# Attention and mixture of depths in one kernel: ranks by one compare, first keys in parts, picks, sums and stores in another order

## The chip, the cores and the metric

The kernel runs on one core of a Trainium2 chip. The metric is the device time of one launch in microseconds (us). Before the change six runs lie between 436.78 and 439.22, median 437.97. The engines of the core work side by side and wait for each other through semaphores: TensorE (PE; its weight loads are shown apart as PEld), VectorE (DVE), ScalarE (ACT), GpSimd (POOL) and SyncE (SP). SP, ACT and POOL also issue DMA transfers, which 16 DMA engines carry out.

## The reference, cut to what matters

All data are float32. With B=8, H=12, S=448, Dh=64, D=768, F=1024, capacity 128:

```python
scores = scale * q @ k.T - log(S)            # for each of 96 heads
attn_out = sigmoid(scores) @ v
x = attn_out as (B, S, H*Dh)
scores = einsum('bsd,d->bs', x, w_gate)      # one gate score per token
out = x.copy()
for b in range(B):
    top_idx = the 128 tokens of 448 with the largest scores[b]
    xe = x[b, top_idx]
    ye = relu(xe @ w1) @ w2
    out[b, top_idx] = xe + sigmoid(scores[b, top_idx])[:, None] * ye
```

## The kernel before, in words

**Attention.** Four heads make a quad; a batch is three quads, so there are 24 quads, handled in pairs: 12 steps s, two quads (x = 0, 1) each. A step has seven slots n = 0..6. In a slot, `score` puts the products of 64 keys and all queries of each head into PSUM with 32x64 tiles of PE, `squash` turns them into sigmoids on ACT (two ACTIVATEs of about 1.0 us), and `value` multiplies earlier sigmoids by v. Scores of one slot and values of earlier slots alternate on PE. In step 0 there are no older values, and the first four slots (0 to 3) hold scores alone: slots 0 and 1 use quad 0, slots 2 and 3 quad 1. In step 0 keys are paired by `chunks` and `column`: pair c < 5 is blocks c and c+5 (a block is 32 tokens), the last four blocks make two pairs of their own.

**Layout.** `load` brings q and k of a quad with a token's row index t and r apart (token = 14 t + r); `turn` transposes 32x32 blocks on DVE, so that the head dimension lies on partitions. `load_v` brings v of both quads of a step: from step 6 on by ACT's queue, issued in slot 3 when the values of the step before are done, because one buffer serves them all; its first use is in slot 4.

**End of a step.** In slot 3 the values of step s-1 are complete. From step 4 on `after(s, 3)` then calls `block(s)`: `takes` (four DVE transposes that free PSUM), the work of the token network listed in `BLOCKS[s]`, which PE does in one go, and then the transposes of the next q and k. In a block, `("t", b)` is `turn_rows`: PE transposes the 128 picked rows of batch b; `(1, p, key)` and `(2, p, key)` are products of the two layers for a pair p of batches. The seven keys are the seven products of a Strassen scheme, which needs sums of weight quarters: `make_sum` builds one on DVE (`MADE` says after which slot), `keep_sum` stores it to DRAM through SP's queue (`KEPT`), `lend` reloads it to a place that is free then (`LENT`).

**Picking rows.** When a batch's output is complete, `gate_part` multiplies a quad's rows by the gate weights and reduces; `gate` adds up, transposes and writes 448 scores to DRAM, `gate_own` keeps each partition's own scores in `who`; `spread` reads the scores back to all partitions (`rep`); `ranking` counts for every token how many scores are above its own: per group of tokens c (`rank`, four groups) one compare with `is_gt` into `above`, and one `is_equal` times the mask `earlier` into `level`. `place` adds both, transposes, writes the ranks to DRAM with four DMAs and reads them back to all partitions (tile `hot`). `fetch` compares the ranks with the partition number, which gives token index and score of each pick, and `gather` fetches the rows of `out` by an indirect DMA. All these DMAs are POOL's; for the last batch SP issues those of `gate`, `spread` and `place`. `RANKED` and `FETCHED` say after which slot; `(5, 3): 1` and others at slot 3 run inside `block`, right after `takes`. `ranking` of odd batches runs in `after(s, 3)` of the step behind.

**Order.** The whole program is emitted by hand (`manual_schedule`): each engine and each queue works off its instructions in the order of the calls. A DMA issue also waits until an earlier DMA of the hardware queues gave back its semaphore.

**The end.** `rest` runs the last products. For batches 6 and 7 (p = 3), `fetch(7)` gathers the last rows, `("t", 7)` turns them, and after the second layer's sums (`second_sums`) `scatter` writes 128 rows back by an indirect DMA.

Of the kernel before, what the change touches and what calls it, by code (L numbers as in the profile page):

```python
# [17 lines left out]
def kernel(  # L18
# [20 lines left out]
    NF = 3  # L39
# [13 lines left out]
    QK_SCALE = 1.0 / math.sqrt(Dh)  # L53
    NEG_LOG_S = -math.log(S)
# [35 lines left out]
    def load(which, *quads):  # L90

        for i in quads:
            if i >= NQ:
                return
            if which == "q":
                t = heads["q", i] = head.tile([P, TB * Dh], F32, name="qT")
            elif i in (1, 2):
                if i == 1:
                    both = heads["both"] = moe.tile([P, 6 * KH * P], F32, name="rows_t")
                t = heads["both"][:, (i - 1) * TB * Dh:i * TB * Dh]  # L100
            else:
                t = head.tile([P, TB * Dh], F32, name="raw_k", bufs=1)
# [4 lines left out]
            heads[which, i] = t  # L107

# [22 lines left out]
    NA = NU - 2  # L131

# [8 lines left out]
    def load_v(s):  # L141
# [4 lines left out]
        if s in (1, 3):  # L146
# [5 lines left out]
        raw_v[s] = t = t.rearrange("p (h c) -> p h c", h=4)  # L152
# [6 lines left out]
        for m in range(4):  # L159
            y, odd = divmod(m, 2)  # L160
            rows = slice(m * TT, (m + 1) * TT)
            if s:
                (nc.scalar if s > 5 else nc.sync).dma_start(
                    out=t[rows], in_=block(y, odd * NU, NU))
            else:
                nc.sync.dma_start(out=t[rows, :, :NA * Dh], in_=block(y, odd * NA, NA))
                nc.sync.dma_start(out=t[rows, :, NA * Dh:],
                                  in_=block(1 - y, 2 * NA + 2 * odd, 2))
# [53 lines left out]
    def keep_sum(m, key):  # L222
# [5 lines left out]
    MADE = {(5, 4): (1, 5), (5, 5): (1, 7), (5, 6): (1, 6), (6, 4): (1, 3),  # L228
            (6, 6): (2, 5), (7, 0): (2, 6), (7, 4): (2, 7), (7, 5): (2, 4)}
    KEPT = {(6, 0): [(1, 5), (1, 7)], (6, 1): [(1, 6)], (6, 5): [(1, 3)],  # L230
            (7, 0): [(2, 5)], (7, 1): [(2, 6)], (7, 5): [(2, 7)], (7, 6): [(2, 4)]}
# [39 lines left out]
    earlier = const.tile([P, NC, S], mybir.dt.uint8, name="earlier")  # L271
# [4 lines left out]
    above = const.tile([P, NC], F32, name="above")  # L276
    level = const.tile([P, NC], F32, name="level")
# [3 lines left out]
    def constants():  # L281
# [10 lines left out]
        nc.gpsimd.memset(above, float(S))  # L292
        nc.gpsimd.memset(level, 0.0)
        for t in (gate_s, place_s, *who):
            nc.gpsimd.memset(t, 0.0)
        mine = moe.tile([P, NC], F32, name="place")
        for a in range(4):
            nc.gpsimd.iota(mine[a * TT:(a + 1) * TT], pattern=[[1, NC]], base=a * NC,
                           channel_multiplier=TB, allow_small_or_imprecise_dtypes=True)
        nc.gpsimd.iota(tokens, pattern=[[1, TB], [TB, TT]], base=0, channel_multiplier=0,  # L300
                       allow_small_or_imprecise_dtypes=True)
        for c in range(NC):
            nc.gpsimd.tensor_scalar(
                out=earlier[:, c, :], in0=tokens.rearrange("p r t -> p (r t)"),
# [740 lines left out]
```

## Time and profile before

| what | us |
|---|---|
| median of six runs | 437.97 |
| the profiled execution, device time | 439.67 |
| its span on the core, first to last instruction | 437.9 |
| PE busy | 423.1 |
| DVE busy | 298.8 |
| ACT busy | 190.7 |
| POOL busy | 52.6 |
| DVE on the two compares of `rank` (L466 and L469; 28 of 32 of each, the last batch is listed apart) | 18.9 and 19.1 |

The profile lists instructions by line of the kernel. A busy PE is not a PE at its full pace: its matmuls overlap, so a matmul that waits for its operands can still lie under the tail of the one before it. Its idle time is therefore a lower bound on what it lost. "Landing" of a DMA is the moment at which its semaphore is complete.

### The profile page before, as it was taken

The page shows a single profiled execution, that of the slowest core. Times are in us where ns is not written, and L with a number is a line of the kernel's source. Part 1 is how long each engine was busy: PE and PEld are TensorE (multiplying, and loading weights), DVE is VectorE, ACT ScalarE, POOL GpSimd, SP SyncE. Part 2 cuts the span into 40 slices and gives each one's busy share as a digit, 9 for nine tenths or more (in the row PEclk, how much of TensorE's full clock was granted, in tenths as well). Part 3 has the DMA queues.
Part 4 walks back from the last instruction along what each step waited for, and adds up shares of the span by engine and source line. Part 5 has one row for each costly group of instructions (what it writes and reads, how often), then busy time and mean ns, then how long its engine had stood idle before and what let it go on. Part 6 is the DMA issues. An engine that isn't in the chain of part 4 may idle for free.

```text
span 437.9 us, 14311 instructions
## 1 busy us (share of the span) xinstructions
PE 423.1 (97%) x6326; PEld 248.9 (57%) x6326; DVE 298.8 (68%) x640; ACT 190.7 (44%) x249; POOL 52.6 (12%) x87
## 2 busy tenths in 40 slices
PE   7999999999998999989999999999999899999995
PEld 3555453535673477455447438646545649768952
DVE  4318467865959975984998566765786768994472
ACT  3766666666653633640660562463263330102000
POOL 6000000210111020020021110010011110101001
PEclk9999999999999999999999999999999999999998
DMA  8786738889944997699649798299875960722001
GB/s 242 223 276 182 234 88 186 183 173 241 278 142 110 231 298 184 167 229 300 185 125 278 238 208 171 88 250 246 211 261 123 193 229 25 148 58 72 37 0 72
DMA packets 114361, 78.64 MB, mean 180 GB/s; under 512 B 91356, under 2 KB 100316, under 8 KB 114300
## 3 DMA queue, kind: packets, MB, share of 16 engines
q1 hardware_dynamic: 107548, 62.70, 54.6%
q0 software_dynamic: 3296, 9.54, 8.0%
q10 hardware_dynamic: 3456, 5.51, 5.0%
q8 instruction: 49, 0.80, 0.7%
q14 instruction: 12, 0.10, 0.1%
HBM read 57.25 MB, written 20.48 MB: 178 GB/s over the span
## 4 chain that ended last, share of the span: by engine, by line
PE 72%; DVE 11%; DMA 10%; issue 3%; ACT 3%; ACTq 1%; POOLq 0%; POOL 0%; SPq 0%; DVEq 0%
PE o L377 26%; PE a L348 26%; PE o L561 7%; PE o L625 5%; PE a L625 4%; DMA raw_v<-in_v_dram 3%; PE a L561 2%; DMA xe<-out_dram,idx 2%; DMA hot<-ranks 2%; ACT attn L362 1%; DVE scr L469 1%; DVE scr L466 1%; DVE scr L493 1%; DVE hidden L574 1%; DVE gate_p L412 1%
## 5 line engine op out<-in xcount | busy, mean ns | idle before, releaser
L348 PE MATMUL a<-qT,kT 32*64 32x448 f32 x2624 | 242.1, 537 | 0.1
L362 ACT ACTIVATE attn<-a,bias_s 128x896 f32<-128x896 f32 x162 | 161.5, 1007 | 84.0 <-PE a L348 81.2
L377 PE MATMUL o<-attn,raw_v 32*64 32x448 f32 x1952 | 175.2, 536 | 0.8 <-DMA raw_v<-in_v_dram 0.6
L348 PEld LDWEIGHTS a<-qT,kT 32*64 32x64 f32 x2624 | 93.9, 131 | 88.4 <-ACT attn L362 52.5
L377 PEld LDWEIGHTS o<-attn,raw_v 32*64 32x64 f32 x1952 | 67.2, 131 | 33.4 <-issue 26.6
L401 DVE STREAM_TRANSPOSE x_b<-o 128x448 f32<-128x448 f32 x48 | 28.1, 626 | 42.3 <-PE o L377 26.1
L377 PE MATMUL o<-attn,rows_t 32*64 32x448 f32 x448 | 42.1, 538 | 0.6 <-issue 0.6
L577 ACT ACTIVATE hidden<-hidden 128x512 f32<-128x512 f32 x12 | 7.5, 630 | 69.2 <-DVE hidden L574 69.2
L412 DVE TENSOR_REDUCE gate_p<-scr 128x14 f32<-128x448 f32 x48 | 29.8, 622 | 1.7
L574 DVE TENSOR_TENSOR hidden<-o,hidden 128x512 f32<-128x512 f32 x23 | 15.2, 687 | 22.4 <-PE o L561 22.2
L409 DVE TENSOR_TENSOR scr<-x_b,wg_b 128x448 f32<-128x448 f32 x48 | 29.4, 612 | 1.0
L329 DVE STREAM_TRANSPOSE kT<-raw_k 128x448 f32<-128x448 f32 x42 | 24.1, 611 | 8.6 <-PE a L348 5.6
L319 DVE STREAM_TRANSPOSE qT<-qT 128x896 f32<-128x896 f32 x22 | 23.7, 1081 | 4.5 <-DMA qT<-in_q_dram 2.8
L481 POOL DMA_DIRECT2D ranks<-turned x28 | 14.5, 524 | 97.5 <-DVE turned L478 97.5
L561 PE MATMUL o<-rows_t,spare 128*128 128x128 f32 x216 | 25.6, 276 | 0.0
L561 PEld LDWEIGHTS o<-rows_t,spare 128*128 128x128 f32 x216 | 24.8, 192 | 1.4 <-DVE x_b L401 1.4
L625 PE MATMUL o<-spare,hidden 128*128 128x384 f32 x72 | 24.3, 488 | 0.0
L636 DVE SCALAR_TENSOR_TENSOR xe<-o,gate,xe 128x384 f32<-128x384 f32 x29 | 16.4, 610 | 9.7 <-PE o L625 9.6
L466 DVE TENSOR_SCALAR_CACHE_REDUCE scr<-rep,who 128x448 f32<-128x448 f32 (+1 forms) x28 | 18.9, 676 | 5.7 <-DMA rep<-scores 4.9
L377 PE MATMUL o<-attn,hidden 32*64 32x448 f32 x224 | 20.6, 538 | 2.1 <-DVE hidden L574 2.1
L377 PEld LDWEIGHTS o<-attn,rows_t 32*64 32x64 f32 x448 | 16.7, 131 | 7.2 <-issue 6.9
L469 DVE SCALAR_TENSOR_TENSOR scr<-rep,who,earlier 128x448 f32<-128x448 f32 (+1 forms) x28 | 19.1, 683 | 1.3
(119 smaller groups left out, 416.7 us busy)
## 6 DMA issues: line engine op xcount, KB each, us to landing
qT<-in_q_dram SPq DMA_DIRECT2D x24, 448.0 KB, 6.3
out_dram<-x_b SPq DMA_DIRECT2D x32, 336.0 KB, 9.1
raw_k<-in_k_dram SPq DMA_DIRECT2D x22, 448.0 KB, 4.4
spare<-sum SPq DMA_DIRECT2D x18, 384.0 KB, 7.4
sum<-spare SPq DMA_DIRECT2D x8, 768.0 KB, 9.4
raw_v<-in_v_dram ACTq DMA_DIRECT2D x24, 224.0 KB, 7.0
w_sb<-in_moe_w_dram SPq DMA_DIRECT2D x6, 768.0 KB, 8.2
rows_t<-in_v_dram SPq DMA_DIRECT2D x8, 224.0 KB, 4.6
```

Of the source, the lines that this page charges most:

```text
L319: nc.vector.transpose(heads["q", i], heads["q", i])
L329: nc.vector.transpose(kt[:, e], t[:, e].rearrange("p (a n) d -> p n a d", a=2))
L348: nc.tensor.matmul(out[y * Dh:(y + 1) * Dh, h % 2, :S], kt[d, e, r:r + 2].rearrange("d r t -> d (r t)"), qt[d, e], start=(e == 0), stop=(e ...
L362: nc.scalar.activation(a, psc[:, :, :S], AF.Sigmoid, bias=bias_s, scale=QK_SCALE)
L377: nc.tensor.matmul(PO[x][pr][j * Dh:(j + 1) * Dh, :S], raw_v[s][rows, 2 * pr + j, at:at + Dh], attn[s, pr, n][rows, j, :], start=((s, x, p ...
L401: nc.vector.transpose(x_tiles[b][:, :, 2 * g + pr, :], PO[x][pr][:, :S].rearrange("p (r t) -> p r t", t=TT))
L409: nc.vector.tensor_tensor(out=tmp, in0=x_tiles[b][:, :, hp, :], in1=wg_b[:, hp:hp + 1, :].to_broadcast([P, TB, TT]), op=ALU.mult)
L412: nc.vector.tensor_reduce(out=gate_parts[b][:, :, hp], in_=tmp, axis=AX.X, op=ALU.add)
L466: nc.vector.tensor_scalar(out=junk[:n], in0=rep[:n], scalar1=own, scalar2=0.0, op0=ALU.is_gt, op1=ALU.add, accum_out=above[:n, c:c + 1])
L469: nc.vector.scalar_tensor_tensor(out=junk[:n], in0=rep[:n], scalar=own, in1=earlier[:n, c, :], op0=ALU.is_equal, op1=ALU.mult, accum_out=l ...
L561: nc.tensor.matmul(ps[:, f, :n], w((t * FH + f) * P, P), x[:, t, :n], start=(t == 0), stop=(t == KH - 1))
L625: nc.tensor.matmul(ps[:n, :DH], h[:, t, :n], w(t * DH, DH), start=(t == 0), stop=(t == FH - 1))
```

## The change

Seven things are changed.

1. **Ranks.** `rank` does one `scalar_tensor_tensor` per group: (other score - own score) > `tie`, summed into `place_s`. `tie` is -2^-126 for tokens of a group that come before the partition's own and 0 elsewhere, so that equal scores within a group rank by order; the gate weights are multiplied by 2^24 once (POOL, in `constants`), and `turn_rows` divides in its sigmoid. `place` then adds equalities between groups with three small `scalar_tensor_tensor` in place of one addition. `above`, `level` and `earlier` are gone; two iotas and one `tensor_scalar` make `tie`.
2. **First loads.** `load_first` replaces the four loads of k and q: of each k the middle eight blocks, then q; then v's first five columns, then the three outer blocks of each side of k, then the rest of v. Keys of step 0 are paired so that slots 0 to 3 need only the middle blocks, and `turn_first` transposes k in three parts. The third of three matmuls on zeros before the first score is gone.
3. **Picks.** `fetch(1)` moves from the block of step 5 (after `takes`) to slot 2 of step 5 (before them); `fetch(2)` from slot (6, 5) to (6, 3), after the transposes of the block. In step 5 the block calls `gate_part` alone; `gate(2)` and `gate_own(2)` follow after the next transposes. `ranking` of odd batches comes before `gates(2s-2)`.
4. **Sums.** `make_sum` of (1, 5) moves from slot (5, 4) to (5, 1). `keep_sum` of (1, 3) moves from (6, 5) to (7, 0), of (2, 7) and (2, 4) from (7, 5) and (7, 6) to (8, 0).
5. **Reload.** The reload of (1, 3) moves from (11, 0) to (11, 4).
6. **End, picking.** In `rest` the ranking of batch 7 comes before `hidden_sum(6)`; its rank DMAs are ACT's; `fetch(7)` comes after the sums of key 4, not 5.
7. **End, storing.** The rows of batch 7 are scattered in two halves of 384 columns, each when its four sums are done.

The core of the diff:

```diff
+    def load_first():
+        for i in range(2):
...
+            for which, src, at, n in (("k", k, AT, TB - 2 * AT), ("q", q, 0, TB)):
+                nc.sync.dma_start(out=raw[which, i][:, at * Dh:(at + n) * Dh], ...)
+        load_v(0, True)
+        for i in range(2):
+            nc.sync.dma_start(
+                out=raw["k", i].rearrange("p (r d) -> p r d", d=Dh)[:, 0:AT],
+                in_=bass.AP(tensor=k.tensor, offset=k.offset + i * 4 * S * Dh,
+                            ap=[[TB * Dh, P], [Dh, AT], [1, Dh]]))
...
+        load_v(0, False)
+    def turn_first(i, *parts):
+        t = heads["raw", i].rearrange("p (r e d) -> p e r d", e=2, d=TT)
+        kt = heads["k", i]
+        for part in parts:
+            if part < 2:
+                nc.vector.transpose(kt[:, :, 2 * part:2 * part + 2],
+                                    t[:, :, AT + part:AT + part + NA + 2:NA + 1])
+                nc.vector.transpose(kt[:, :, 2 * (NA + part):2 * (NA + part) + 2],
+                                    t[:, :, NA + part:NA + part + 3:2])
+                continue
+            for a, r in ((0, 0), (1, TB - AT)):
+                nc.vector.transpose(kt[:, :, 4 + a:2 * NA:2], t[:, :, r:r + AT])
-    MADE = {(5, 4): (1, 5), (5, 5): (1, 7), (5, 6): (1, 6), (6, 4): (1, 3),
+    MADE = {(5, 1): (1, 5), (5, 5): (1, 7), (5, 6): (1, 6), (6, 4): (1, 3),
-    KEPT = {(6, 0): [(1, 5), (1, 7)], (6, 1): [(1, 6)], (6, 5): [(1, 3)],
-            (7, 0): [(2, 5)], (7, 1): [(2, 6)], (7, 5): [(2, 7)], (7, 6): [(2, 4)]}
+    KEPT = {(6, 0): [(1, 5), (1, 7)], (6, 1): [(1, 6)], (7, 0): [(1, 3), (2, 5)],
+            (7, 1): [(2, 6)], (8, 0): [(2, 7), (2, 4)]}
-        nc.vector.tensor_scalar(out=junk[:n], in0=rep[:n], scalar1=own, scalar2=0.0,
-                                op0=ALU.is_gt, op1=ALU.add, accum_out=above[:n, c:c + 1])
-        nc.vector.scalar_tensor_tensor(
-            out=junk[:n], in0=rep[:n], scalar=own, in1=earlier[:n, c, :],
-            op0=ALU.is_equal, op1=ALU.mult, accum_out=level[:n, c:c + 1])
+        nc.vector.scalar_tensor_tensor(
+            out=junk[:n], in0=rep[:n], scalar=own, in1=tie[:n],
+            op0=ALU.subtract, op1=ALU.is_gt, accum_out=place_s[:n, c:c + 1])
     def place(b):
-        queue = nc.sync if b == B - 1 else nc.gpsimd
-        nc.vector.tensor_add(place_s[:, :NC], above, level)
+        queue = nc.scalar if b == B - 1 else nc.gpsimd
+        for c in range(NC - 1):
+            nc.vector.scalar_tensor_tensor(
+                out=place_s[:, c + 1:NC], in0=who[b % 2][:, c + 1:NC],
+                scalar=who[b % 2][:, c:c + 1], in1=place_s[:, c + 1:NC],
+                op0=ALU.is_equal, op1=ALU.add)
+    def scatter_half(b, m):
+        nc.gpsimd.indirect_dma_start(
+            out=out[:b + 1].rearrange("b s (m d) -> (b s m) d", m=2),
+            out_offset=bass.IndirectOffsetOnAxis(ap=st[b]["halves"][m][:n, 0:1], axis=0),
+            in_=st[b]["xe"][:n, m * DH:(m + 1) * DH], in_offset=None)
-            (11, 0): [(1, 3, "heads"), (2, 4, "heads")],
+            (11, 0): [(2, 4, "heads")], (11, 4): [(1, 3, "heads")],
     def block(s):
-        if (s, NF) in FETCHED:
+        if (s, NF) in FETCHED and s > NF + 3:
             fetch(FETCHED[s, NF])
-        if s in FULL[::2]:
+        if s == NF + 2:
+            gate_part(2 * s - 2)
+        elif s in FULL[::2]:
             gates(2 * s - 2)
     def rest():
-        first_sums(*begin((1, p, 3), bank()), sums_too=(5, 6))
-        work = {key: begin((2, p, key), bank()) for key in (2, 1, 4)}
-        ranking(b)
+        first_sums(*begin((1, p, 3), bank()), sums_too=(5,))
+        ranking(b)
+        hidden_sum(p, 6)
+        work = {key: begin((2, p, key), bank()) for key in (2, 1, 4)}
-            if key == 5:
+            if key == 4:
                 fetch(b)
     def after(s, n):
+            if s == NF + 2:
+                gate(2)
+                gate_own(2)
+            if s == NF + 3:
+                fetch(FETCHED[s, NF])
+            if s - 1 in FULL[1::2]:
+                ranking(FULL.index(s - 1))
             if s not in FULL[::2]:
                 gates(2 * s - 2)
-            if s - 1 in FULL[1::2]:
-                ranking(FULL.index(s - 1))
-    FETCHED = {(3, 6): 0, (5, 3): 1, (6, 5): 2, (8, 3): 3, (9, 5): 4, (11, 3): 5}
+    FETCHED = {(3, 6): 0, (5, 2): 1, (6, 3): 2, (8, 3): 3, (9, 5): 4, (11, 3): 5}
     def stream():
-        for cols in (4 * P, 4 * P, 2 * P):
+        for cols in (4 * P, 4 * P):
```

## The prediction

> **What bounds the kernel now.** I read the page first, then PE's own waits, the chain that ended last in order of time, and the timelines of DVE, POOL and SP around each place where PE waits.
>
> ```profile
> PE 423.1 (97%) x6326; PEld 248.9 (57%) x6326; DVE 298.8 (68%) x640; ACT 190.7 (44%) x249; POOL 52.6 (12%) x87
> ...
> DMA  8786738889944997699649798299875960722001
> ```
>
> PE is the bound, but not at its full pace. In steady state eight 32x64 matmuls start every 0.375 us, a product of the first layer takes 2.68 us and one of the second 2.58 (chain). 5376 matmuls at 0.047, 28 products of each kind and eight row turns of 0.8 give 252.0 + 147.3 + 6.4 = 405.7. The span is 437.9, so some 32 us are start, end and waits. DMA is the other tight resource: 9 tenths in many slices.
>
> PE's waits, longest first (us in total, times, longest):
>
> ```profile
> PE o L377 <- DVE hidden L574: 2.1, 1, 2.1
> PE o L526 <- DVE hidden L608: 1.6, 1, 1.6
> ...
> PE o L526 <- DMA xe<-out_dram,idx: 1.2, 1, 1.2
> PE a L526 <- DMA attn<-out_dram,idx: 0.9, 1, 0.9
> PE p L348 <- DVE qT L324: 0.8, 2, 0.4
> ...
> PE o L377 <- DMA raw_v<-in_v_dram: 0.6, 1, 0.6
> ```
>
> These are idle times; measured from one matmul's start to the next, less the usual pitch, the same places lose 2.6, 1.7, 1.35, 1.0, about 1.5 (two starts) and 1.5 (two starts). The chain (start, us) shows where:
>
> ```profile
> 5.50 0.54 DVE qT L324
> 6.08 1.78 PE p L348 x32
> ...
> 123.73 5.24 DMA hot<-ranks
> ...
> 132.49 0.63 DVE gate_p L412
> 135.79 0.70 DVE hidden L574
> ...
> 231.77 11.32 DMA raw_v<-in_v_dram
> ...
> 336.84 8.32 DMA xe<-out_dram,idx
> ...
> 394.02 3.76 DMA attn<-out_dram,idx
> ...
> 428.68 3.01 DMA out_dram<-xe,idx
> ```
>
> The wait at 194.75 is named after L608, an addition that has nothing to do with the rows turned. The indirect DMA does:
>
> ```profile
> 186.07 0.15 DVE L496 TENSOR_SCALAR idx<-got 128x1 int32<-128x1 f32 x1
> 186.49 2.27 POOL L508 DMA_INDIRECT xe<-out_dram,idx  x1 [3.60 <-DVE idx L496]
> 196.58 0.52 PE L526 MATMUL o<-iden,xe 128*128 128x128 f32 x3 [1.55 <-DVE hidden L608]
> ```
>
> It landed at 196.44, 0.14 before PE went on, the same distance as at 345.16 and 397.78. So the reader sees six places, each with a different cause; what the change does at each is the forecast.
>
> **The change part by part** (times are those of the trace before).
>
> *Ranks.* A compare is 0.68 to 0.69 with a pitch of 0.72; four fewer save 2.9 per batch, 23 us of DVE in all. Three small operations at a pitch of 0.2 (L476 0.16) replace one: +0.4. Net 2.5 per batch. DVE's idle time elsewhere swallows this where it isn't named below. The iotas and `tie` are POOL's, which made masks until 8.6 (4 x 1.4) and is idle until 64; scaling `wg_b` waits there for a DMA of about 13 us, long before step 1's gates: nothing.
>
> *Start: 0.6.* First matmul at 6.08 = q's landing (about 5.25) + half a transpose of q, with k's four transposes from 4.21 to 5.43 in front. After: k's middle is 256 KB of 448. The packets of 3584 B run at about 400 GB/s here, so q lands 0.5 earlier, at 4.75; two transposes of 128 columns (pitch 0.19) are hidden before it. PE starts at about 5.45, and the zero matmuls, 0.86 apiece, end at 4.9 instead of 5.65. ACT then sets the pace (eight ACTIVATEs without a gap from 7.88), so the 0.6 carries on if quad 1's q lands by 8.4; it did at 8.88 and has two half k's less in front, about 7.9. Slot 4 needs the outer k at about 13.0. They are issued as ninth to twelfth DMA, each when an earlier one landed, the last at about 7.9. Nearest rows for their packets: 512-byte ones took 44 ns and 128-byte ones 14, against 196 for 3584; that makes their 384 KB 2.1 to 2.7 us instead of 1.3, behind v's 640 KB. I expect 11.5 to 12.5 plus four small transposes. Bounds: 1.0 (q alone limits) and -0.3 (they land at 14).
> The Trainium skill, "DMA: Bandwidth & Descriptors", section "Why small descriptors are slow (HBM only)", speaks against splitting k: it gives a 256-byte descriptor 27% overhead. By that the outer keys would cost about 1.7 us, by the rows 2.1 to 2.7; either way the start keeps its cover.
>
> *Step 5, 133.9: 2.6.* `(1, 0, 2)` ends on PE at 132.5, its addition L574 waits on DVE until 135.79 behind `fetch(1)` (which waited for `hot` until 128.97), `gate_part`, `gate` and `gate_own` (133.15 to 135.76). PE needs that PSUM for values at 133.96 and got it at 136.53; ACT's late sigmoid costs 0.54 more at 138. After: takes end at 128.4, `gate_part` at 131.0, addition 132.55 to 133.25. Gain 3.1. In exchange `fetch(1)` stands ahead of `takes`, so PE's product at 127.1 now waits for `hot` if it is late. Ranks start at 109.2 instead of 111.78 and end after 2.9 + 0.6 + 0.4 at 113.1 (118.35 before). Before, from there to `hot` it took 10.6. So 123.8, fetch until 125.4, and takes start at 125.76 for PE anyway. But the ranks' DMAs now run in a busier stretch:
>
> ```profile
> 109.50:120.40 10.90, 10.90 (x237) 6.73 (x229) 9.96 (x26) 6.66 (x7) 1.75 (x4) 1.00 0.91 279
> 120.40:131.40 11.00, 11.00 (x183) 8.09 (x168) 6.13 (x14) 6.17 (x9) 1.41 (x3) 1.00 0.46 141
> ...
> 153.30:164.20 10.90, 10.90 (x132) 7.89 (x117) 8.28 (x17) 4.17 (x9) 2.62 (x5) 1.00 0.97 297
> ```
>
> (DMA share and GB/s at the end of a line.) In the third stretch the same path took 16.0 (154.24 to 170.22). PE loses one for one after 125; I take 12.4, a cost of 0.5. Bounds 0 and 4.5 (by the 16.0). `make_sum` (1, 5), 1.75, moves ahead of that fetch; its weights land at 120.4, so it ends by 122.5, inside the wait. `gate(2)` and its two POOL DMAs come some 4 us later against PE; batch 2's ranking starts at 148.3, its scores are back by about 144.5: nothing.
>
> *Step 7, 194.75: 1.6.* `fetch(2)` runs at about 175 (its `hot` landed at 170.2, stores of batch 2 at 173.6) instead of 184.74. Even the slowest gather, 9.95, lands by 187. The 1.6 of DVE time delays gates and sums in between but the queue up to 190.8 has the same total. On POOL the gather passes the scores DMA of batch 3; nobody is late. Bounds 1.7 and 0 (if POOL waits for a store).
>
> *Step 8, 241: 1.3.* v of step 8 is issued by ACT at 229.3 to 232.2 and lands at 243.1, after q, q, k and a 768 KB sum that SP could only issue between 224.4 and 229.4, since SP stood before the store of (2, 7) for DVE. After: q and q go at about 217; k waits for its transpose (about 225) and the two sums follow. In front of v are then k and two sums, about 5.6 us of the DMA engines by their packets (8 of 0.18, 16 of 0.26) from 227 on; v's own 4.2 finishes at about 237 to 239, PE wants it at 241. The (1, 3) store behind (7, 0)'s loads frees SP the same way. Bounds 1.5 and 0 (sums still in the way).
>
> *Last picks, 397: 0.9.* Ranking of batch 7 starts 0.7 earlier (`hidden_sum(6)` goes behind it; its reader, key 6, starts on PE about 387) and is 2.5 shorter: end at 382.7, not 385.9. Then four issues and a read back, `hot` at 389 to 390.5 instead of 391.65; fetch no longer has key 5's sums in front. Rows at 395.5 to 396.8, PE wants them at 396.9. Behind the fetch wait the sums of keys 5, 6, 7; their banks are needed at 393.9 and 396.8, and they are done by 393.2 and 396. ACT has nothing else until 391.5. Bounds 1.0 and 0.
> For the change of queue, "DMA: Bandwidth & Descriptors", section "Issuing engines are not separate DMA queues", says that only issue time is saved, here nothing; the trace shows ACT issuing v alone.
>
> *Last store: 0.4.* The last scatter's packets moved for about 1.1 us of its 3.0; half as many bytes save 0.4. The first half is issued on POOL at 431.2 for 1.0, clear of 433.84. Bounds 0.6 and 0.
>
> *Reload of (1, 3), step 11: -0.5.* It now enters SP's queue between the stores of batch 6, whose issues run from 333.25 to 345.5, while `gather(5)` (8.32 us, 1.35 late) and v are under way. 768 KB are 2.1 us of the DMA engines. Its reader comes after 370. Bounds 0 and -2.0.
>
> *What is late next: -0.4.* Moving PE forward by 3 at 134 leaves the next v (step 6, last packet 171.46, wanted at about 171.7) no slack, in a stretch with DMA at 0.97. SP's queue there is triggered by DVE's transposes, which move forward too, so I take a small part. Bounds 0 and -2.0.
>
> Sum: 0.6 + 2.6 + 1.6 + 1.3 + 0.9 + 0.4 - 0.5 - 0.4 = 6.5. The profiled execution took 439.67 with a span of 437.9, 1.7 above the median; its waits are taken as those of the median run, so 437.97 - 6.5 = 431.5.
>
> **The rivals.**
> *DMA takes it back.* For: 0.91 to 0.97 in the stretches behind step 5, the 0.2 us of slack at 171.5. Against: the requests move forward with PE. Step 5's gain less 2, step 8's gain gone: 6.5 - 2.0 - 1.3 = 3.2, 434.8.
> *The change doesn't do what it says.* DVE, 68% busy, isn't the bound, so shorter ranks and earlier picks only move idle time, and start and end alone count: 0.6 + 0.4, 437.0. Against: four of the six waits hang on DVE's order.
> *Slower: `fetch(1)` before `takes`.* Place: DVE at 124, ahead of PE's product at 127.1. Price: one for one once `hot` lands after 125. All else being 3.9 and step 5's 3.1 being at stake, it decides from 132 on, and for 0.3% more from 133.3: 20 us from the ranks, against 10.6 and 16.0 seen. At 134: 439.
>
> **How the numbers follow.** 0.3%, or 1.3 us, is about what can be told from no change here. Forecast 0.71 (428.8 to 433.8), DMA takes it back 0.13, nothing but the ends 0.08, slower 0.08. The low end is the sum of the upper bounds (1.0 + 3.1 + 1.7 + 1.5 + 1.0 + 0.6 = 8.9, 429.1, less a little); the high end takes in the first rival and part of the second, 436.8. Faster 0.83, same 0.09, slower 0.08.
>
> **What would show it.** Right: first score matmul near 5.5; no L574 wait in PE's list around 130; row turns of batches 2 and 7 without a wait; v of step 8 there before PE; DVE busy about 20 us less (298.8 to 279). Wrong: DVE waiting for `hot` at L493 ahead of the takes of step 5; a PE wait on `raw_v` at steps 6 or 8; PE's wait for batch 5's rows growing past 2.

## The result, and the profile after

The changed kernel takes 436.22 us (median of 32 runs, 433.68 to 439.55), the kernel before measured beside it 438.85 (74 runs, 434.95 to 442.05). The ratio is 0.9941, 95% interval 0.9927 to 0.9956. The change is faster by 2.6 us; the forecast was 6.5. The ratios in this document compare undisturbed runs of the two kernels alone, so they can differ by 0.1 to 0.2% from the quotient of the medians.

The two profiled executions lie further apart than the medians: 434.81 after against 439.67 before, 4.9 us (spans 433.0 and 437.9). Executions of one kernel spread over 6 to 7 us, so a single pair can be some 2 us off, and this one is. From the page of after, the busy times and the DMA's tenths:

```profile
PE 421.8 (97%) x6324; PEld 252.6 (58%) x6324; DVE 281.6 (65%) x598; ACT 190.6 (44%) x249; POOL 48.9 (11%) x82
...
DMA  7787737999963998989566887399835991921001
```

DVE's busy time fell by 17.2 us, 298.8 to 281.6. PE's waits of after (us in total, times, longest):

```profile
PE p L391 <- DVE qT L375: 2.0, 2, 1.7
PE p L1077 <- DVE bias_s L1069: 1.4, 1, 1.4
PE o L423 <- ACT attn L405: 0.5, 1, 0.5
PE o L580 <- DVE x_b L447: 0.3, 1, 0.3
```

The waits that the forecast was made of, at steps 5, 7 and 8, for batch 5's rows and for the last rows, are all gone. One at the start has grown: 1.7 us for the q of the second quad.

To find where time went, take the first ACTIVATE of a slot as a mark and measure from mark to mark. (5,3) is slot 3 of step 5. These are differences of start times in the profiled executions, in us; PE's last matmul is taken at its start. The other columns are experiments described below.

| stretch | before | before, once more | ranks alone | ranks and picks | ranks and picks, once more | whole change |
|---|---|---|---|---|---|---|
| start of span to (0,4) | 16.58 | 16.79 | 16.61 | 16.73 | 17.26 | 17.37 |
| step 5, (5,3) to (5,4) | 11.05 | 11.47 | 10.27 | 8.12 | 8.12 | 8.46 |
| (5,4) to (6,3) | 18.65 | 19.98 | 18.65 | 18.75 | 18.75 | 18.75 |
| step 6, (6,3) to (6,4) | 16.55 | 16.60 | 17.44 | 16.77 | 16.55 | 17.41 |
| step 7, (7,3) to (7,4) | 18.04 | 17.60 | 16.89 | 16.86 | 16.37 | 16.37 |
| step 8, (8,3) to (8,5) | 18.31 | 17.12 | 16.70 | 16.47 | 16.46 | 16.46 |
| step 11, (11,3) to (11,4) | 15.28 | 15.32 | 14.08 | 13.93 | 13.90 | 14.02 |
| (11,6) to PE's last matmul | 78.44 | 78.92 | 77.40 | 77.38 | 77.39 | 77.39 |
| PE's last matmul to end of span | 5.46 | 5.46 | 5.41 | 5.41 | 5.41 | 6.96 |
| span | 437.88 | 439.96 | 434.83 | 431.02 | 429.06 | 433.02 |

Between before and the whole change: step 5 gives 2.6, step 7 1.7, step 8 1.85, step 11 1.3, the last picks 1.05. Step 6 costs 0.9, the start 0.8, the end 1.5. That is a gain of 5.3; the remaining stretches take 0.4, which makes the pair's 4.9. Step 11 isn't named as a gain by the forecast at all.

Step 5 on DVE, as forecast (timeline of after; start, duration, engine, line, what it does, idle time and releaser in brackets):

```profile
119.76 1.72 DVE L270 TENSOR_TENSOR spare<-spare,w_sb 128x1536 f32<-128x1536 f32 x1
124.84 0.68 DVE L541 SCALAR_TENSOR_TENSOR scr<-hot,slot_s,tokens 128x448 f32<-128x448 f32 x1 [3.36 <-DMA hot<-ranks]
...
126.37 1.18 DVE L447 STREAM_TRANSPOSE x_b<-o 128x448 f32<-128x448 f32 x2
...
133.81 0.69 DVE L629 TENSOR_TENSOR hidden<-o,hidden 128x512 f32<-128x512 f32 x1 [2.33 <-PE o L616]
```

The sum (1, 5) sits inside the wait for `hot`, the fetch is done before `takes`, and the addition of the layer (L629) now waits for PE instead of PE for it.

The end, on POOL (timeline of after), is where the forecast had the wrong sign:

```profile
422.32 0.97 POOL L705 DMA_INDIRECT out_dram<-xe,idx  x1 [23.87 <-DVE xe L691]
426.11 0.96 POOL L713 DMA_INDIRECT out_dram<-attn,idx  x1 [2.82 <-DMA out_dram<-xe,idx]
429.39 0.97 POOL L713 DMA_INDIRECT out_dram<-attn,idx  x1 [2.32 <-DMA out_dram<-attn,idx]
```

Three scatters in a row: batch 6, and the halves of batch 7 (L713). Each is issued only when the one ahead of it has landed; all three write `out`. DVE had the last half ready at about 427.2. Before, the single last scatter waited 4.19 us for DVE (`attn`) and for no DMA.

### The profile page after: what moved, and what is told of

Read it like the earlier page. It is cut to its first block, busy times and chain, and to the rows that moved or that the text cites. A ratio compares the mean times of both kernels' runs of the same rounds, so it can differ in the third digit from the quotient of the medians.

```text
span 433.0 us, 14255 instructions
## 1 busy us (share of the span) xinstructions
PE 421.8 (97%) x6324; PEld 252.6 (58%) x6324; DVE 281.6 (65%) x598; ACT 190.6 (44%) x249; POOL 48.9 (11%) x82
## 4 chain that ended last, share of the span: by engine, by line
PE 93%; DMA 3%; ACT 1%; issue 1%; DVE 0%; SPq 0%; POOLq 0%; ACTq 0%
PE a L391 30%; PE o L423 29%; PE o L616 11%; PE o L680 11%; PE a L616 6%; PE a L680 5%; DMA qT<-in_q_dram 2%; PE o L580 1%; ACT attn L405 1%; DMA out_dram<-xe,idx 1%; DMA out_dram<-attn,idx 1%; PE p L391 0%; PE a L580 0%; SPq L120 0%; POOLq L1117 0%
## 5 line engine op out<-in xcount | busy, mean ns | idle before, releaser
L391 PEld LDWEIGHTS a<-qT,kT 32*64 32x64 f32 x2624 | 95.2, 131 | 86.3 <-ACT attn L405 52.0
L423 PEld LDWEIGHTS o<-attn,raw_v 32*64 32x64 f32 x1952 | 69.6, 131 | 29.5 <-issue 23.3
L629 DVE TENSOR_TENSOR hidden<-o,hidden 128x512 f32<-128x512 f32 x23 | 15.2, 688 | 24.8 <-PE o L616 24.6
L455 DVE TENSOR_TENSOR scr<-x_b,wg_b 128x448 f32<-128x448 f32 x48 | 29.6, 616 | 1.1
L513 DVE SCALAR_TENSOR_TENSOR scr<-rep,who,tie 128x448 f32<-128x448 f32 (+1 forms) x28 | 19.0, 677 | 8.8 <-DMA rep<-scores 8.1
L616 PE MATMUL o<-rows_t,w_sb 128*128 128x128 f32 x168 | 20.0, 276 | 0.2 <-issue 0.2
```

The source lines that it names most:

```text
L391: nc.tensor.matmul(out[y * Dh:(y + 1) * Dh, h % 2, :S], kt[d, e, r:r + 2].rearrange("d r t -> d (r t)"), qt[d, e], start=(e == 0), stop=(e ...
L423: nc.tensor.matmul(PO[x][pr][j * Dh:(j + 1) * Dh, :S], raw_v[s][rows, 2 * pr + j, at:at + Dh], attn[s, pr, n][rows, j, :], start=((s, x, p ...
L455: nc.vector.tensor_tensor(out=tmp, in0=x_tiles[b][:, :, hp, :], in1=wg_b[:, hp:hp + 1, :].to_broadcast([P, TB, TT]), op=ALU.mult)
L513: nc.vector.scalar_tensor_tensor(out=junk[:n], in0=rep[:n], scalar=own, in1=tie[:n], op0=ALU.subtract, op1=ALU.is_gt, accum_out=place_s[:n ...
L616: nc.tensor.matmul(ps[:, f, :n], w((t * FH + f) * P, P), x[:, t, :n], start=(t == 0), stop=(t == KH - 1))
```

## The experiments

The first three, and the ranks alone, were compared on one chip, the next four on one, the last four on one; each ratio is against runs of the kernel before in the same comparison (medians 440.35, 440.22 and 437.55).

**One last scatter instead of two halves, in the changed kernel.**

```diff
-            if b == B - 1:
-                parts = st[b].setdefault("parts", [4, 4])
-                ...
-                    scatter_half(b, m)
-            elif not left[x]:
+            if not left[x]:
```

> The changed kernel with the last batch's rows written by one indirect DMA again, when all eight sums are done. In the changed kernel's profile the first half waited on POOL for the scatter of batch 6 to land (issue 426.11) and the second for the first half (issue 429.39, though its sums ended at 427.2); it landed at 431.95. Theory (the halves wait for each other): one scatter is issued at about 427.5 and lands 3.0 later, at 430.5, so 1.5 us faster than the changed kernel, ratio to the kernel before about 0.9905. Rival (the halves cost nothing, the missing gain is lost in the middle): the same as the changed kernel within 0.3 us, ratio 0.994.

Measured: 436.01 us, ratio 0.9887 (0.9824 to 0.995). From PE's last matmul to the end of the span 5.42 us instead of 6.96. The 1.5 at the end are the halves', as the theory had it; by the medians alone, whose intervals overlap, it would not be shown.

**The old start in the changed kernel.**

```diff
-        load_first()
+        for i in range(2):
+            load("k", i)
+            load("q", i)
+        load_v(0)
...
-        for cols in (4 * P, 4 * P):
+        for cols in (4 * P, 4 * P, 2 * P):
```

(and the old pairing and transposes with it.)

> The changed kernel with the first loads, key pairs, transposes and the three zero matmuls of the kernel before. Theory (the start turned from a gain of 0.6 into a loss of 0.8, because q of quad 1 lands at 9.7 instead of 8.9): third slot's scores start at 9.7 instead of 10.5, and the kernel is 0.8 to 1.4 us faster than the changed one (0.5 of it by a later wait around 44 us that the changed kernel has), ratio to the kernel before 0.991 to 0.9925. Rival (the late q is an accident of one execution, the start does gain 0.6): 0.6 slower than the changed kernel, ratio 0.9955.

Measured: 437.85 us, ratio 0.9936 (0.9903 to 0.997), the same as with the new start. (0,4) begins at 16.90 instead of 17.37. No gain of the new start shows, and no loss either at this resolution; neither the theory nor the rival is confirmed.

**Both together: old start and one scatter.**

> The changed kernel with the old start and with one scatter at the end: ranks, picks, sums, reload and last picks as changed. Theory (two terms of the sum had the wrong sign, the waits in the middle are as forecast): 2.3 to 2.9 us faster than the changed kernel, ratio to the kernel before 0.9875 to 0.989. Rival (the gains in the middle are taken back by the DMA engines and the ends are neutral): 0.994.

Measured: 435.55 us, ratio 0.989 (0.9845 to 0.9935), within the interval of one scatter alone. (0,4) begins at 17.25 here with the old start, so the spread of that mark is as large as what is looked for.

**The ranks alone, in the kernel before.** One compare per group with `tie` and scaled weights (part 1 of the change), nothing else.

```diff
-        nc.vector.tensor_scalar(out=junk[:n], in0=rep[:n], scalar1=own, scalar2=0.0,
-                                op0=ALU.is_gt, op1=ALU.add, accum_out=above[:n, c:c + 1])
...
-            out=junk[:n], in0=rep[:n], scalar=own, in1=earlier[:n, c, :],
-            op0=ALU.is_equal, op1=ALU.mult, accum_out=level[:n, c:c + 1])
+            out=junk[:n], in0=rep[:n], scalar=own, in1=tie[:n],
+            op0=ALU.subtract, op1=ALU.is_gt, accum_out=place_s[:n, c:c + 1])
```

> The kernel before with the ranks changed alone (one compare per group, three small operations between groups, scaled gate weights). Theory (DVE is not the bound; only where a wait of PE hangs on DVE behind a ranking does it count): at step 5 the ranks are read back 2.5 us earlier, so the pick ends before 129 and PE's wait for L574 shrinks from 2.6 by up to 1.2 (DVE then waits for the end of the takes at 128.4); the last rows come about 1 us earlier: 1.0 to 2.2 us faster, ratio 0.995 to 0.998. Rival (shorter ranks carry the whole gain): 4 us or more, ratio under 0.991. Second rival (they do nothing alone): 1.0 within 0.001.

Measured: 435.36 us, ratio 0.9893 (0.9843 to 0.9943), no less than the whole change gains. The theory missed (0.995 to 0.998); the rival that the shorter ranks carry the whole gain came out. PE's waits of this kernel:

```profile
PE o L377 <- DVE hidden L576: 1.3, 1, 1.3
...
PE o L377 <- DMA raw_v<-in_v_dram: 0.2, 1, 0.2
```

The wait for DVE in step 5 has shrunk from 2.1 to 1.3, and there is none left for batch 2's rows (step 7), for batch 5's or for the last ones, though `fetch(2)`, the stores and the last picks stand where they stood. The last gather is issued earlier because its ranks are: 37.6 us after (11,6) instead of 40.0. The gathers of batches 2 and 5 are not: they are issued 30.4 us after (6,3) and 4.15 after (11,3) in both kernels, but they land sooner, batch 2's after 7.1 us instead of 9.95, batch 5's after 7.1 instead of 8.3. Why they take less time is not shown. At step 8 the stores of the weight sums, and behind them the two q, are issued 2.8 us earlier, counted from (8,3), since DVE, done with batch 3's ranking sooner, makes the last sums at 219.7 instead of 222.6. So the gains that the forecast gave to the moves of steps 7 and 8 and of the end come for the most part with the shorter ranks.

**The kernel before, once more,** unchanged, to see which of its waits recur.

> The kernel before once more, unchanged, for a second profile of it. Theory (the long ranks cause the waits): PE waits again at the turn of batch 2 (step 7, 1.7), for v at step 8 (1.5), for the rows of batch 5 (step 11, 1.35) and of batch 7 (1.0), each within 0.5, beside the 2.6 at step 5. Rival (the transfers of one execution): at least two of the four are under 0.5 this time, since nothing but the timing of the DMA engines differs.

Measured: 439.29 us, ratio 0.9983 (0.9943 to 1.0024). PE's waits in its profiled execution:

```profile
PE o L377 <- DVE hidden L574: 2.5, 1, 2.5
PE o L526 <- DMA xe<-out_dram,idx: 1.7, 2, 1.2
PE p L1000 <- DVE bias_s L994: 1.4, 1, 1.4
PE a L526 <- DMA attn<-out_dram,idx: 1.3, 1, 1.3
```

Steps 5 and 11 and the last rows recur. For batch 2's rows (step 7) PE waits 0.5 instead of 1.6: their gather took 8.9 us, not 9.95. The wait for v at step 8 does not recur: there its last part landed 13.6 us after (8,3) instead of 14.8, PE was not idle for it, and (8,3) to (8,5) took 17.12 instead of 18.31. So two thirds of step 8's 1.85 belonged to the one execution that was read.

**The old ranks in the changed kernel** (two compares per group, everything else as changed).

> The changed kernel with the two compares per group back, all else as changed. Theory (the shorter ranks carry most of the gain): 2 to 4 us slower than the changed kernel, ratio to the kernel before 0.998 to 1.003; at step 5 the scores of the ranks are read back 2.5 us later, at about 127.3, so the takes wait for the pick and PE waits about 3 us at its product near 127. Rival (picks, sums, reload and last picks carry it, as forecast): 0.5 to 1 us slower than the changed kernel, ratio 0.995 to 0.9965.

Measured: 447.44 us, ratio 1.0183 (1.0127 to 1.0239): slower than before by 8 us, far more than theory or rival. DVE around step 5, and PE's waits:

```profile
123.75 1.72 DVE L269 TENSOR_TENSOR spare<-spare,w_sb 128x1536 f32<-128x1536 f32 x1
129.27 0.69 DVE L540 SCALAR_TENSOR_TENSOR scr<-hot,slot_s,tokens 128x448 f32<-128x448 f32 x1 [3.80 <-DMA hot<-ranks]
...
130.67 0.64 DVE L447 STREAM_TRANSPOSE x_b<-o 128x448 f32<-128x448 f32 x1
```

```profile
PE o L579 <- DVE x_b L447: 3.0, 2, 2.7
PE o L579 <- DMA xe<-out_dram,idx: 2.6, 1, 2.6
...
PE o L614 <- DVE x_b L447: 2.3, 1, 2.3
```

`hot` lands at 129.2 instead of 124.7, `takes` stand behind the fetch and begin only at 130.67, and PE waits 2.3 us for them (L614). Even so (5,3) to (5,4) takes 10.45, less than the 11.05 of before. Most of the loss is in step 6, 21.06 instead of 16.55: the takes are late again (2.7), now behind the ranking of batch 2, which waits for its scores until 154.1 (before it starts at 148.3), because `gate(2)` has moved; then the granted clock falls (last section). The gather of batch 5 takes 9.7 us and costs 2.6. Without the short ranks the rest of the change is a loss.

**Ranks and picks in the kernel before**: parts 1 and 3, that is the short ranks, `fetch(1)` and `fetch(2)` earlier, `gate(2)` later, ranking ahead of the gates.

```diff
-    FETCHED = {(3, 6): 0, (5, 3): 1, (6, 5): 2, (8, 3): 3, (9, 5): 4, (11, 3): 5}
+    FETCHED = {(3, 6): 0, (5, 2): 1, (6, 3): 2, (8, 3): 3, (9, 5): 4, (11, 3): 5}
...
+            if s == NF + 2:
+                gate(2)
+                gate_own(2)
+            if s == NF + 3:
+                fetch(FETCHED[s, NF])
```

> The kernel before with the ranks and the picks changed (fetch of batches 1 and 2 earlier, gate of batch 2 later, ranking ahead of the gates), without the sums, reload, last picks, start and halves. Theory: 4.7 from the ranks alone (measured, interval 2.5 to 6.9) and up to 2.2 more at step 5 (10.27 to about 8.3 between its third and fourth sigmoid), of which step 6 takes back some 0.5 in waits for v: 5 to 6.5 faster than the kernel before, ratio 0.985 to 0.989. Rival (what step 5 gains is taken back by the DMA engines at steps 6 to 8): no faster than the ranks alone, 0.989 to 0.991.

Measured: 433.91 us, ratio 0.9859 (0.9817 to 0.9901). Step 5 takes 8.12 instead of the 10.27 of the ranks alone and the 11.05 of before; no wait for a row or for v is left. This is within the theory's range.

**Longer ranks in the kernel before**: the first compare done twice, 2.9 us of DVE more per batch.

```diff
+        junk = moe.tile([P, S], F32, name="scr")
+        nc.vector.tensor_scalar(out=junk[:n], in0=rep[:n], scalar1=own, scalar2=0.0,
+                                op0=ALU.is_gt, op1=ALU.add, accum_out=above[:n, c:c + 1])
```

> The kernel before with the first compare of every group done twice: 12 compares per batch in place of 8, 2.9 us of DVE more per batch, the same result. Theory (DVE's time in the ranks is on PE's path at several places): about the mirror image of the shorter ranks, 3 to 5 us slower, ratio 1.007 to 1.011; the wait at step 5 grows by 2.4 to 2.9 and that of the last rows by 2.9. Rival (the ranks are covered, only the last batch's counts): 1 to 3 us slower, at the last rows alone, with step 5 unchanged.

Measured: 450.96 us, ratio 1.0224 (1.0175 to 1.0273), some 10 us longer, twice the theory's 3 to 5: it is no mirror image. DVE is busy for two thirds of the span only, and yet 23 us of additional work on it cost 10 and 20 us less gain about 5: several places of the program hang on when the ranks are done.

```profile
PE o L377 <- DVE hidden L577: 5.3, 1, 5.3
PE a L529 <- DMA attn<-out_dram,idx: 2.0, 1, 2.0
```

The wait of step 5 grows from 2.1 to 5.3, that for the last rows from 0.9 to 2.0. (5,3) to (5,4) is 3.2 longer than before, the stretch behind it 1.6 (the clock, last section), (11,6) to PE's last matmul 2.4, step 8 1.2.

The last four kernels all contain the short ranks and the picks, and add one further part each; the first is the base.

**Ranks and picks, once more.**

> The kernel before with the new ranks and picks, once more, as the base of the other three on the same chip. Theory: 0.984 to 0.989 times the kernel before, as the first time (0.986); from PE's last matmul to the end 5.4 us; step 5 from slot 3 to slot 4 about 8.1. Rival (the first median was a favourable one): 0.99 or above.

Measured: 431.83 us (429.99 to 434.45), ratio 0.9874 (0.9826 to 0.9922), as the theory had it.

**... with the last store in halves.**

> The kernel before with the new ranks and picks, plus the last store in two halves. Theory (the second half waits for the landing of the first): from PE's last matmul to the end of the span 6.9 to 7.05 us instead of 5.4, and a median 1.5 above that of ranks and picks alone (433.9 in the other comparison, so about 435.4). Rival (the wait is a matter of one execution, or something later hides it): no difference over 0.5. The prediction's own term would put it 0.4 below.

Measured: 434.12 us (432.11 to 436.37), ratio 0.9923 (0.9892 to 0.9955), 2.3 above the base. From PE's last matmul to the end of the span it is 6.97 us against 5.41, and each half again waits for the landing ahead of it (POOL's timeline):

```profile
424.98 0.97 POOL L667 DMA_INDIRECT out_dram<-attn,idx  x1 [2.82 <-DMA out_dram<-xe,idx]
428.27 0.97 POOL L667 DMA_INDIRECT out_dram<-attn,idx  x1 [2.32 <-DMA out_dram<-attn,idx]
```

1.56 of the 2.3 are thus shown; the rest is within the spread of the runs.

**... with the new start.**

> The kernel before with the new ranks and picks, plus the new first loads (keys paired otherwise, k in parts, two zero matmuls). Theory (the first score comes 0.5 earlier, but q of the second quad lands later, so nothing is left): within 0.5 of ranks and picks alone, about 433.9; the start of step 0's fifth slot at 16.7 to 17.4 us. The prediction's own term: 0.6 below, about 433.3. Rival (the new start is part of what the full change gives back): 0.8 to 1.5 above, with step 0's fifth slot at 17.4 or later.

Measured: 432.89 us (431.74 to 435.12), ratio 0.9893 (0.9847 to 0.9939), 1.1 above the base, which by itself is less than the intervals tell apart; it lies in the rival's range, not in the theory's. (0,4) begins at 17.05 against 17.26. What the prediction had not looked at comes after it. In this execution (0,4) to (1,0) took 10.76 instead of 9.48 us; DVE and then PE there:

```profile
22.11 1.11 DVE L370 STREAM_TRANSPOSE qT<-qT 128x896 f32<-128x896 f32 x1 [0.73 <-DMA qT<-in_q_dram]
24.72 1.11 DVE L370 STREAM_TRANSPOSE qT<-qT 128x896 f32<-128x896 f32 x1 [1.50 <-DMA qT<-in_q_dram]
25.83 0.06 DVE L433 MEMSET o<- 1x1 f32 x2
```

```profile
25.89 0.59 PE L391 MATMUL a<-qT,kT 32*64 32x448 f32 x2 [0.70 <-DVE o L433]
```

q of step 1 is late, DVE waits for it, and a small MEMSET that PE needs stands behind. The reason is SP's queue, where the new start puts four more loads (the outer keys) ahead of step 1's: SP issues step 1's two q from 16.59 on,

```profile
16.59 0.91 SPq L103 DMA_DIRECT2D qT<-in_q_dram  x2
```

and in the base from 14.18 on. In the other three executions with the new start it issues them at 15.56 to 16.55; so lateness of that size costs something in some of them only. Of the four profiled executions with the new start two show this (10.76, and 10.57 with the old ranks) and two have 9.48 there; all ten with the old start have 9.48.

**... with the moved weight sums and the moved reload** (parts 4 and 5).

> The kernel before with the new ranks and picks, plus the moves of the weight sums, their stores and the reload. Theory (with short ranks v of step 8 comes in time without these moves, so they bring nothing and cost at most what step 6 shows, 0.4): 433.9 to 434.4, with no gain from slot (8, 3) to (8, 5). The prediction's own terms (1.3 for the moved sums, -0.5 for the reload): 0.8 below, about 433.1. Rival (they cost what lies between the two medians measured apart, 435.5 with and 433.9 without them): 1 to 1.6 above.

Measured: 433.63 us (431.89 to 436.06), ratio 0.9906 (0.9873 to 0.9939), 1.8 above the base. (8,3) to (8,5) takes 16.46, as without the moves: they gain nothing once the ranks are short. The 1.8 is at the rival's end. Step 11 took 15.69 instead of 13.90, with this wait of PE:

```profile
PE o L528 <- DMA xe<-out_dram,idx: 1.6, 1, 1.6
```

The gather of batch 5 was issued at 331.71 and landed at 340.45, after 8.7 us; in the base it took 6.8 (330.4 to 337.2). In the four other executions with the moved reload step 11 lies between 14.01 and 14.22, 0.1 to 0.3 above the base, and once, with the old ranks, at 16.69.

## Why the prediction was wrong, by its own steps

The sign was right, the size was 2.5 times too large, and 436.22 lies just inside the stated range. These steps failed: "Last store: 0.4" (measured -1.5), "Start: 0.6" (at best nothing), the sentence that idle time swallows the shorter ranks (4.7 us come from them alone), and the last step, which took the waits of one execution for those of the median run (2.2 of the missing 3.9).

Nearly all that was to show the forecast right came true: the first score at 5.48, no wait for the addition in step 5, the row turns without a wait, v of step 8 in time, DVE 17 us less busy. Of the signs of being wrong one came, DVE's wait for `hot` ahead of the takes (3.36 us), at no cost. None of these signs tells what the last scatters and the second quad's q cost.

**Ranks.** The count was right: compares, their accumulator reads and `place` took 50.0 us of DVE before and take 29.6 now, 2.5 per batch (single durations added up; accumulator reads overlap compares, so DVE's busy time fell by less, 17.2). Groups of instructions of after:

```profile
L513 DVE SCALAR_TENSOR_TENSOR scr<-rep,who,tie 128x448 f32<-128x448 f32 (+1 forms) x28 | 19.0, 677 | 8.8 <-DMA rep<-scores 8.1
L521 DVE SCALAR_TENSOR_TENSOR place_s<-who,place_s 128x3 f32<-128x3 f32 (+2 forms) x24 | 5.3, 221 | 0.8
```

The sentence "DVE's idle time elsewhere swallows this where it isn't named below" failed. The ranks alone give 0.9893, and the kernel with all the rest and the old ranks 1.0183. Most of what was credited to moves is theirs, and step 11, which the forecast doesn't name as a gain, went from 15.28 to 14.08 with them alone.

**Step 5: 2.6.** 2.6 in the profiled pair. 0.8 come with the ranks alone, the rest with the picks. `hot` landed at 124.7, forecast 123.8 and, with the surcharge, 125.6. That the later `gate(2)` costs "nothing" was too simple: batch 2's ranking waits for its scores until 150.5 (forecast: back by about 144.5) and ends at 154.1, right before the takes of step 6 begin. With the short ranks it just fits; with the old ones it is the 2.7 us of that kernel.

**Step 7: 1.6.** 1.7 measured, but 1.15 of it with the ranks alone, where batch 2's gather is issued no earlier and lands sooner. **Step 8: 1.3.** 1.85 in the pair, 0.7 against the second execution of before, and 0.4 to 0.7 of it without any moved store; the moves themselves give nothing. **Last picks: 0.9.** 1.05 measured, all of it with the ranks alone; another order, another queue and an earlier fetch add nothing, as the same 77.4 stands in four columns.

**Last store: 0.4.** This term failed in its sign: -1.5. The forecast saw that half as many bytes land sooner (2.5 instead of 3.0 us, which holds) and that the first half is clear of the second in POOL's time. It overlooked that a scatter into `out` waits for the landing of the scatter ahead of it. The trace of before had shown it, at the two scatters of batches 4 and 5 (POOL's timeline):

```profile
405.14 0.99 POOL L645 DMA_INDIRECT out_dram<-xe,idx  x1 [2.87 <-DMA out_dram<-xe,idx]
```

With 3.0 + 0.8 from batch 6's issue to the first half's and 2.5 + 0.8 to the second's, the sum could have been made: 422.32 + 3.8 + 3.3 = 429.4, against DVE's 427.2 plus 0.3. Landing at 429.4 + 2.5 = 431.9 against 427.5 + 3.0 = 430.5 for one scatter gives a loss of 1.4.

**Start: 0.6.** The first score did move, 6.08 to 5.48, but PE then waited 1.7 us for the second quad's q:

```profile
9.69 1.17 DVE L375 STREAM_TRANSPOSE qT<-qT 128x448 f32<-128x448 f32 x2 [1.48 <-DMA qT<-in_q_dram]
```

It landed at about 9.7; the forecast's condition was 8.4, its guess 7.9, and before it was 8.88. In the pair 0.8 are lost at (0,4), outside the bounds of -0.3 to 1.0; over all profiled executions that mark lies at 17.10 on the average of four with the new start and 16.92 of ten with the old, so the start is at best even. The forecast reckoned only with what is issued ahead of that q, while in the trace v's packets of 1280 bytes, issued behind it, ran among its last ones. It also left out what is pushed back: four loads more on SP ahead of step 1's q. The premise of the 256-byte rule was wrong as well: in the trace the three outer blocks move in packets of 768 bytes, so the price of the Trainium skill, "DMA: Bandwidth & Descriptors", section "Why small descriptors are slow (HBM only)", did not come into play; slot 4 did not wait for the outer keys. Nor do the 196 ns taken for packets of 3584 bytes show: in the first 9 us before they took 163 on average and mostly 140; only the estimate for the outer keys rests on it.

**Reload: -0.5.** Against kernels without the moved reload it costs 0.1 to 1.8, on the average of the five executions with the short ranks about 0.5 (13.90 against 14.42). The term fits that average, which one execution of 1.8 makes. What it left out is that step 11 gains 1.3 with the ranks: the gather of batch 5, issued 4.15 us after (11,3) in all of these, takes 6.8 to 7.1 us without the moved reload and 8.3 before. The runs don't show why.

**What is late next: -0.4.** 0.9 in step 6, within the bounds; the ranks alone show the same 0.9, ranks and picks 0.2 and nothing; it differs from execution to execution.

So of the profiled pair's 4.9: the terms for steps 5 to 8 and the last picks brought 6.3 with step 6's loss, close to their 6.0; step 11 brought 1.8 more than its term; the end took 1.9 and the start 1.4 more than theirs, and 0.4 went in stretches without a term (6.5 + 0.3 + 1.8 - 1.9 - 1.4 - 0.4 = 4.9). What remains between 4.9 and 2.6 is the last step of the working: "its waits are taken as those of the median run". The execution read of before lay 0.8 above the median of 74 runs, that of after 1.4 below its own, and step 8's wait was not there in a second execution. Six runs had put before at 437.97, the larger number puts it at 438.85.

**The rivals.** "The change doesn't do what it says" rested on DVE not being a bound, and fell: 20 us less of DVE's work made the kernel 4.7 us faster, 23 us more made it 10 slower. "DMA takes it back" shows in step 6 alone, and there by 0 to 1.3 us from execution to execution. "Slower: `fetch(1)` before `takes`" named a real mechanism: with the old ranks in the changed kernel, `hot` lands at 129.2 and PE waits 2.3 us for the takes. But step 5 is still shorter there than before, so this isn't what makes that kernel 8 us slower; the rival did not name step 6, where most of it lies.

**What the parts are worth.** The short ranks give some 4.7 us (2.5 to 6.9). The picks bring it to 5.5 to 6.2 in two comparisons; the intervals overlap those of the ranks alone, but step 5 shows 2.15 us of it (10.27 to 8.12). The halves, and with less certainty the start and the sums with the reload, give back what lies between that and 2.6. The lowest ratios are those of ranks and picks alone: 0.9859 and 0.9874 of the time before, against 0.9941 (0.9927 to 0.9956) for the whole change. That it beats the whole change is clear of the intervals; that it beats the changed kernel with one scatter is not. How much of the loss beyond the halves' 1.5 belongs to the start and how much to the reload is not settled: 1.1 and 1.8 are known to 2 or 3 either way, and with the halves' 2.3 they add up to 5.2 where some 3.2 are to be explained (0.9941 less the 0.9867 between the two comparisons, of 438).

## What to carry to other kernels

An engine that is 68% busy can set the pace wherever the bound engine waits for something that stands behind it in order; cost a shorter operation at every such place, before crediting the moves that come with it. A gather that lands earlier need not have been issued earlier: measure both from the same mark. Before splitting a transfer, look in the trace at what the queue waited for between two transfers into the same tensor, and count for each load put ahead in a queue what is then issued later. Read at least two executions before a wait of 1 us is put into the sum as a gain.

## What the runs showed of the hardware that was not expected

**A wait costs more than its idle time.** After PE's wait in step 5 the granted clock fell. Stretches (us; then sum, busy PE, PEld, DVE, ACT, POOL; granted clock, DMA share, GB/s) of the second execution of before,

```profile
134.00:137.40 3.40, 0.90 (x24) 0.12 (x8) 3.09 (x14) 0.00 (x1) 0.55 (x1) 1.00 0.28 98
137.40:142.00 4.60, 4.58 (x64) 2.41 (x72) 4.53 (x7) 2.79 (x5) 0.56 (x1) 0.64 0.47 99
```

and of the kernel with longer ranks:

```profile
136.00:142.00 6.00, 0.77 (x19) 0.00 (x0) 5.58 (x19) 0.00 (x0) 1.75 (x2) 0.79 0.25 66
142.00:146.50 4.50, 4.48 (x56) 1.87 (x64) 4.43 (x7) 2.88 (x5) 0.56 (x1) 0.53 0.42 101
```

2.5 us idle were followed by 0.64 over 4.6 us, 5.3 us idle by 0.53 over 4.5. In narrower stretches the clock is 0.50 from 138.7 to 142.1 in the first, 3.4 us, and from 139.5 to 146.2 in the second, about twice that, with 1.00 on either side. The row (5,4) to (6,3) prices it: 19.98 and 20.26 instead of 18.65, 1.3 and 1.6 us. The first profiled execution of before was idle for 2.1 us at the same place and kept a clock of 1.00. With the old ranks in the changed kernel a wait of 2.7 us in step 6 was followed by 0.50 from 161.2 to 164.5, one of 2.6 us in step 11 by 1.00: the length of the pause alone does not decide. So the wait of step 5 was worth up to 1.3 us more than the 2.6 forecast, in some executions. The Trainium skill, "TensorE: Matmul & The Clock Gate", section "Part 1: The HAM clock gate (the "warmup" mystery)", describes a free-running activity window of about 3.4 us, which lets the clock depend on how a pause falls into the window; that agrees with the 3.4 us at 0.50 here, and with a drop after 2.5 and 2.7 us and none after 2.1 and 2.6.

**The first score is not steady.** Its 32 matmuls took 1.76 us in the two profiles compared, and between 1.76 and 2.70 in the others (2.70 with one scatter, 2.43 with the sums). The trace's record of the granted clock begins with the full clock, and at different times: at 5.07 us before, 5.26 after, 7.34 with one scatter, 7.45 with the sums (the 1.00 that a stretch ahead of the first record shows has no record behind it). Where the first score begins ahead of that time, eight of its matmuls take about 0.8 us at first and 0.38 afterwards. In all fourteen profiles the duration is within 0.05 us of 1.76 plus half the time that the record begins after the first matmul. So the slow matmuls ran at half the clock. The full clock came at 4.32 to 7.58 us behind two matmuls on zeros and at 4.87 to 7.45 behind three, so the third made no difference that these profiles show; the end of the first score scatters by up to 0.9 us for it.
